# Decode attention with hand-written semaphores: TensorE's chunks as turns of one loop, V in one fixed buffer

## The chip, the cores and the metric

One core of a Trainium2 chip. The metric is the device time of one execution in microseconds (us), the median over runs; lower is better. "Before" is the kernel as it was, "changed" the rewritten one. The profile counts 16 DMA engines for the core, and the trace records 16 increments of each load's semaphore; each is taken here as the moment at which one engine's part of the load has arrived, and is called a landing. VectorE is DVE in the profile, ScalarE is ACT, GpSimd is POOL, and SP is the engine that issues most loads.

## The reference, cut to what matters

```python
def _A_ref(x, k_cache, v_cache, wq, wo):             # one token, D = 448
    q = (x @ wq) ...                                  # 16 heads of 256; 8 K/V heads, 65536 positions
    scores = einsum("bhqd,bhkd->bhqk", q, k) * (256 ** -0.5)
    p = softmax(scores)
    o = einsum("bhqk,bhkd->bhqd", p, v)
    return o @ wo
def _B_ref(x, w1, b1, w2, b2): ...                    # a small token mixer with gelu
return g * a + (1 - g) * b                            # g: one sigmoid gate
```

K and V are bf16, 8 x 65536 x 256 each: 2 x 268 MB, read once. Everything else is small (Wq and Wo are 3.7 MB each).

Of the kernel before, what the change touches and what calls it, by code (L numbers as in the profile page):

```python
# [21 lines left out]
RING = 3  # L22
MAXS = max(SIZES)


PAD = MAXS - 1
# [6 lines left out]
GELU_C1 = 0.044715  # L33


@with_exitstack
def kernel(
# [24 lines left out]
    assert DR == 64 and D % 4 == 0 and F % 128 == 0 and SK % (128 * SB * sum(SIZES)) == 0  # L62
    sizes = SIZES * (SK // (128 * SB * sum(SIZES)))
    n_chunks = len(sizes)
    n_steps = HKV * sum(sizes)
    scale = 1.0 / (DH ** 0.5)

    ctx.enter_context(tc.manual_schedule())


# [3 lines left out]
    work = ctx.enter_context(tc.tile_pool(name="work", bufs=1))  # L74
# [3 lines left out]
    ring = [ringp.tile([128, MAXS * SB * DH], BF16, name=f"ring{i}") for i in range(RING)]  # L78

    sc = [psum.tile([128, 512], FP32, name=f"sc{i}") for i in range(2)]  # L80
    pv = [psum.tile([128, 512], FP32, name=f"pv{i}") for i in range(2)]
    misc = psum.tile([128, 512], FP32, name="misc")
    den_ps = psum.tile([128, 512], FP32, name="den_ps")

    acc = psum.tile([128, 512], FP32, name="acc")


    total = HKV * n_chunks

    def piece(item, j, n):  # L90
        i, is_v = divmod(item, 2)
        g, c = divmod(i, n_chunks)
        nb = sizes[c] * SB
        lo = sum(sizes[:c]) * SB * 128
        src = (A_v_cache if is_v else A_k_cache)[0, g, lo:lo + 128 * nb, :]
        src = src.rearrange("(p j) d -> p (j d)", j=nb)
        nc.sync.dma_start(
            out=ring[item % RING][:, j * DH:(j + n) * DH], in_=src[:, j * DH:(j + n) * DH]
        )

    def load(item):
        last = sizes[-1]
        if item < 2 * total - 2:
            piece(item, 0, sizes[item // 2 % n_chunks] * SB)
        elif item == 2 * total - 1:

            for s in range(last):
                piece(item - 1, s * SB, SB)
            for s in range(last - 1):
                piece(item, s * SB, SB)  # L110
            piece(item, (last - 1) * SB, SB - TAIL)
            piece(item, last * SB - TAIL, TAIL)



    wq_slot = ring[RING - 1]
    wqa = wq_slot[:, 0:KA * HQ * DH].rearrange("p (k n) -> p k n", k=KA)
    wqb = wq_slot[:, KA * HQ * DH:KA * HQ * DH + 8 * DH]
    nc.sync.dma_start(
        out=wq_slot[:, 0:KA * HQ * DH], in_=A_wq[0:DA, :].rearrange("(p k) n -> p (k n)", k=KA)  # L120
    )
    nc.sync.dma_start(out=wqb, in_=A_wq[DA:D, :].rearrange("r (hh n) -> (r hh) n", hh=2))
    for item in range(RING - 1):
        load(item)


    x_row = const.tile([1, D], BF16)
    nc.scalar.dma_start(out=x_row[:], in_=A_x[0])
    gw_row = const.tile([1, D], BF16)
    nc.scalar.dma_start(out=gw_row[:], in_=gate_w.rearrange("(o n) -> o n", o=1))  # L130
    w1T = const.tile([128, NF], FP32)
    nc.gpsimd.dma_start(out=w1T[:], in_=B_w1[0, :].rearrange("(p b) -> p b", b=NF))
    b1T = const.tile([128, NF], FP32)
    nc.gpsimd.dma_start(out=b1T[:], in_=B_b1.rearrange("(p b) -> p b", b=NF))
    w2T = const.tile([128, NF], BF16)
    nc.gpsimd.dma_start(out=w2T[:], in_=B_w2[:, 0].rearrange("(p b) -> p b", b=NF))
    zb = const.tile([1, 2], FP32)
    nc.gpsimd.dma_start(out=zb[:, 1:2], in_=B_b2.rearrange("(o n) -> o n", o=1))

    wo_t = [const.tile([128, 4, D], BF16, name=f"wo{i}") for i in range(2)]  # L140

    def load_wo(g):
        nc.gpsimd.dma_start(  # L143
            out=wo_t[g % 2][:],
            in_=A_wo[g * 512:(g + 1) * 512, :].rearrange("(q p) n -> p q n", p=128),
        )


    ident = const.tile([128, 128], BF16)
    make_identity(nc, ident[:])  # L150



    sel = const.tile([128, 4], FP32)
    classes = sorted(set(sizes), reverse=True)
    assert list(sizes) == sorted(sizes, reverse=True)
    pick = const.tile([128, 2, len(classes)], FP32)
    nc.gpsimd.memset(sel[:], 0.0)
    nc.gpsimd.memset(pick[:], 0.0)
    rows = [(sel[:], 4, -1, 32 * a) for a in range(4)]  # L160
    for k, size in enumerate(classes):
        rows += [(pick[:, :, k], 2, -16, 32 * a + s) for a in range(4) for s in range(size)]
    for t, w, step, row in rows:
        nc.gpsimd.affine_select(  # L164
            out=t, in_=t, compare_op=ALU.not_equal, fill=1.0, base=-row,
            pattern=[[step, w]], channel_multiplier=1,
        )
    block = const.tile([128, 4], FP32)
    nc.gpsimd.memset(block[:], 0.0)
    for a in range(4):  # L170
        nc.gpsimd.memset(block[32 * a:32 * a + 32, a:a + 1], 1.0)
    mhalf = const.tile([128, 1], FP32)
    nc.gpsimd.memset(mhalf[:], -0.5)

    pairs = const.tile([128, 2, 256], BF16)
    nc.vector.memset(pairs[:, 0, :], 0.0)
    nc.vector.memset(pairs[:, 0, 0:256:2], 1.0)
    nc.vector.transpose(out=pairs[:, 1, :].bitcast(FP32), in_=pairs[:, 0, :].bitcast(FP32))
    one_b = pairs[0:1, 1, 0:256:2]
    one_f = const.tile([1, 128], FP32)  # L180
    nc.vector.memset(one_f[:], 1.0)

    kT = [work.tile([128, SB * DH], BF16, name=f"kT{i}") for i in range(2)]
    p_t = [work.tile([128, 512], BF16, name=f"p{i}") for i in range(2)]
    pT_t = [work.tile([128, 512], BF16, name=f"pT{i}") for i in range(2)]
    den = [work.tile([128, n_chunks], FP32, name=f"den{i}") for i in range(2)]
    dsum = work.tile([128, len(classes)], FP32, name="dsum")
    rden = work.tile([128, 2], FP32, name="rden")
    pvs = work.tile([128, 512], FP32, name="pvs")
    oT = work.tile([128, 4], BF16, name="oT")  # L190
    half_g = work.tile([128, 1], FP32, name="half_g")
    bias = work.tile([128, 1], FP32, name="bias")
    res = work.tile([128, DQ], BF16, name="res")
    qT = const.tile([128, 2, HQ], BF16)
    qr = const.tile([128, 8, HQ], BF16)
    qw = [const.tile([128, 8, WIN], BF16, name=f"qw{i}") for i in range(2)]
    gate = const.tile([128, 2], FP32)

    for t in pv + qw:
        nc.vector.memset(t[:], 0.0)  # L200
    nc.vector.memset(acc[:, 0:DQ], 0.0)


    xd = const.tile([1, 2, 128], BF16)
    nc.vector.memset(xd[:], 0.0)
    for hh in range(2):
        nc.vector.tensor_copy(
            out=xd[:, hh, :].rearrange("o (r two) -> o r two", two=2)[:, :, hh],
            in_=x_row[:, DA:D],
        )  # L210
    x_ps = misc[:, 480:480 + KA + 2]
    for k in range(KA + 2):
        if k < KA:
            row = x_row[:, 0:DA].rearrange("o (p k) -> o p k", k=KA)[:, :, k]
        else:
            row = xd[:, k - KA, :]
        nc.tensor.matmul(x_ps[:, k:k + 1], lhsT=row, rhs=one_b[:, 0:1], start=True, stop=True)
    xT = const.tile([128, KA + 2], BF16)
    nc.vector.tensor_copy(out=xT[:], in_=x_ps)


    u_b = work.tile([128, D], FP32, name="u_b")
    xg = u_b[0:1, :]
    nc.vector.tensor_tensor(out=xg, in0=x_row[:], in1=gw_row[:], op=ALU.mult)
    nc.vector.tensor_reduce(out=zb[:, 0:1], in_=xg, axis=AXIS.X, op=ALU.add)
    z_ps = misc[:, 500:502]
    nc.tensor.matmul(z_ps, lhsT=one_f[:], rhs=zb[:], start=True, stop=True)  # L227
    nc.scalar.activation(out=gate[:, 0:1], in_=z_ps[:, 0:1], func=ACT.Exp, scale=-1.0)
    nc.scalar.activation(out=gate[:, 1:2], in_=z_ps[:, 0:1], func=ACT.Exp, scale=1.0)  # L229
    nc.vector.tensor_scalar(out=gate[:], in0=gate[:], scalar1=1.0, scalar2=None, op0=ALU.add)  # L230
    nc.vector.reciprocal(out=gate[:], in_=gate[:])
    nc.vector.tensor_scalar(
        out=half_g[:], in0=gate[:, 1:2], scalar1=0.5, scalar2=None, op0=ALU.mult
    )
    nc.vector.tensor_tensor(out=bias[:], in0=z_ps[:, 1:2], in1=gate[:, 1:2], op=ALU.mult)


    xb_ps = sc[0][:, 0:D]
    nc.tensor.matmul(xb_ps, lhsT=one_b, rhs=x_row[:], start=True, stop=True)
    stats = const.tile([128, nc.vector.BN_STATS_DIM], FP32)  # L240
    nc.vector.bn_stats(out=stats[:], in_=xb_ps)
# [57 lines left out]

    queries(0)  # L300
    load(RING - 1)
    load_wo(0)
    load_wo(1)


# [212 lines left out]
```

## The kernel before: what the change and the argument touch

Each K/V head is cut into 6 chunks of 6, 6, 5, 5, 5, 5 steps; a step is 16 x 128 positions. A chunk of K or V is one load of 5 or 6 MiB, all from SP's queue, into a ring of three buffers that K and V share. TensorE's stream is unrolled over all 48 chunks; a framework places the semaphores.

```python
RING = 3
ring = [ringp.tile([128, MAXS * SB * DH], BF16, name=f"ring{i}") for i in range(RING)]
...
# K and V alternate: item 2i is K of chunk i, item 2i+1 is V of chunk i
nc.sync.dma_start(out=ring[item % RING][:, ...], in_=src[:, ...])
...
for i in range(total):                       # 48 chunks, all unrolled
    g, c = divmod(i, n_chunks)
    for s in range(sizes[c]):
        turn(i, s, n)                        # VectorE transposes one step of K (128x2048 fp32 words)
        scores(i, s, n)                      # TensorE: 8 matmuls 128x512
        mixer(n)
        ...
    load(2 * i + RING)                       # V of i+1: its buffer is free after scores(i)
    softmax(i)                               # ScalarE exp, VectorE transpose
    for s in range(...):
        p_v(i, s)                            # TensorE: 8 matmuls 4x512
    load(2 * i + 1 + RING)                   # K of i+2: its buffer is free after p_v(i)
```

The last V arrives in pieces. The last of its five steps is multiplied in a "turned" form (weights from V, output 128x2), which adds to the folded p.V of all steps before it in PSUM. Then come Wo, a bias and the output.

The softmax here doesn't subtract the row's maximum and nothing guards it: scores larger than these inputs give would overflow.

## Time and profile before

| | before |
|---|---|
| time | 1273.83 us (3 runs, 1273.68 to 1273.90) |
| span of the profiled run | 1272.2 us |
| bytes moved | 544.90 MB, 428 GB/s over the span |
| busy: TensorE / VectorE / DMA queue of K and V | 57% / 49% / 98.5% |
| instruction blocks: 16384 bytes / second queue | 35 / 11 |
| landings of the last load (16 engines) | 1259.4 to 1267.6 us, mean 1263.5 |

The page of the kernel before, first its share of busy time, then DMA by fortieths of the span and by queue (packets, MB, share of 16 engines' span):

```profile
PE 723.6 (57%) x4552; PEld 285.1 (22%) x4552; DVE 626.8 (49%) x388; ACT 58.4 (5%) x149; POOL 78.5 (6%) x145
...
DMA  9999999999999999999999999999999999999997
GB/s 408 426 428 433 432 439 429 429 432 433 435 432 431 431 433 435 431 432 431 432 438 429 432 433 437 435 425 435 431 435 436 427 432 435 436 438 425 432 429 301
...
q1 hardware_dynamic: 15416, 540.55, 98.5%
q0 software_dynamic: 1376, 3.69, 0.8%
q8 instruction: 35, 0.57, 0.2%
q14 instruction: 11, 0.09, 0.0%
```

No compute engine is near its limit and the DMA engines are never idle. The 35 packets on q8 are instructions. And the last slice, 301 GB/s, is where the engines end one by one.

The end of the kernel before, in order of time (start us, duration, engine, source line, operation):

```profile
1265.25 0.81 PE L382 MATMUL pv<-ring,pT 128*4 128x512 bf16 x8 [0.26 <-DMA ring<-in_A_v_cache_dram]
...
1266.11 0.42 DVE L472 COPY pvs<-pv 128x256 f32<-128x256 f32 x1 [3.32 <-PE pv L382]
1266.57 0.38 ACT L473 ACTIVATE pvs<-pv 128x256 f32<-128x256 f32 x1 [5.69 <-DVE pvs L472]
...
1266.59 1.05 PE L414 MATMUL misc<-sel,pvs 128*128 128x2 f32 x8 [0.54 <-DVE pvs L472]
...
1267.51 0.97 PE L425 MATMUL misc<-pT,ring 128*128 128x2 bf16 x32
...
1269.51 0.65 SPq L485 DMA_DIRECT2D out_dram<-res  x1
```

The last piece lands at 1267.6 us; the output is issued 1.9 us after that landing.

### The profile page before, as it was taken

Reading aid. Unit: us, or ns where it says so; the run is one execution under the profiler, and the core shown is the slowest. Engines: PE = TensorE matmul, PEld = TensorE weight load, DVE = VectorE, ACT = ScalarE, POOL = GpSimd, SP = SyncE. Lnnn points to the kernel's source line nnn. Section 1 sums busy time; section 2 is a strip of 40 time slices with the busy share of each in tenths; the row PEclk is TensorE's granted clock in tenths of the full one; section 3 lists DMA queues with packets and bytes.
Section 4 is the critical chain, followed back from the end, with each engine's and each line's share of the span. In section 5 each row is a group of like instructions: output and inputs, shape, how many; then the busy total and the mean of one; then the engine's idle time right before and its main releaser. Section 6 shows DMA issues by size and latency. Waiting matters only on the chain.

```text
span 1272.2 us, 10454 instructions
## 1 busy us (share of the span) xinstructions
PE 723.6 (57%) x4552; PEld 285.1 (22%) x4552; DVE 626.8 (49%) x388; ACT 58.4 (5%) x149; POOL 78.5 (6%) x145
## 2 busy tenths in 40 slices
PE   1566556654666546564565646655465555665467
PEld 1222122221222112221222212222122212222123
DVE  2555354644555355453554445544455435544455
ACT  0000000000000000000000000000000000000000
POOL 4110101111011110110000000000000000000000
PEclk9978777888788877888778888888788887878778
DMA  9999999999999999999999999999999999999997
GB/s 408 426 428 433 432 439 429 429 432 433 435 432 431 431 433 435 431 432 431 432 438 429 432 433 437 435 425 435 431 435 436 427 432 435 436 438 425 432 429 301
DMA packets 16842, 544.90 MB, mean 428 GB/s; under 512 B 2202, under 2 KB 2332, under 8 KB 3484
## 3 DMA queue, kind: packets, MB, share of 16 engines
q1 hardware_dynamic: 15416, 540.55, 98.5%
q0 software_dynamic: 1376, 3.69, 0.8%
q8 instruction: 35, 0.57, 0.2%
q14 instruction: 11, 0.09, 0.0%
q10 hardware_dynamic: 4, 0.00, 0.0%
HBM read 544.22 MB, written 0.00 MB: 428 GB/s over the span
## 4 chain that ended last, share of the span: by engine, by line
DMA 63%; PE 17%; DVE 11%; issue 8%; ACT 1%; POOL 0%; DVEq 0%; ACTq 0%; SPq 0%; POOLq 0%
DMA ring<-in_A_k_cache_dram 59%; PE sc L359 12%; DVE kT L351 9%; PE pv L382 5%; DMA zb<-in_B_b_dram 2%; DMA ring<-in_A_v_cache_dram 2%; DVE pT L370 1%; ACT p L366 1%; PE den_ps L398 0%; PE misc L270 0%; DVEq L351 0%; PE acc L314 0%; PE misc L414 0%; PE misc L274 0%; PE misc L425 0%
## 5 line engine op out<-in xcount | busy, mean ns | idle before, releaser
L359 PE MATMUL sc<-kT,qw 128*128 128x512 bf16 x2048 | 575.7, 434 | 443.8 <-DVE kT L351 442.8
L351 DVE STREAM_TRANSPOSE kT<-ring 128x2048 f32<-128x2048 f32 x256 | 575.3, 2288 | 478.1 <-DMA ring<-in_A_k_cache_dram 396.1
L359 PEld LDWEIGHTS <-qw 128*128 128x128 bf16 x2048 | 215.5, 108 | 791.5 <-DVE kT L351 332.2
L382 PE MATMUL pv<-ring,pT 128*4 128x512 bf16 x2040 | 125.7, 395 | 62.1 <-DVE pT L370 61.8
L370 DVE STREAM_TRANSPOSE pT<-p 128x512 bf16<-128x512 bf16 x48 | 34.2, 712 | 130.9 <-ACT p L366 130.9
L382 PEld LDWEIGHTS <-pT 128*4 128x4 bf16 x2040 | 46.6, 89 | 135.0 <-DVE pT L370 81.7
L366 ACT ACTIVATE p<-sc 128x512 bf16<-128x512 f32 x48 | 28.7, 597 | 1037.6 <-PE sc L359 1037.6
L143 POOL DMA_DIRECT2D wo<-in_A_wo_dram x8 | 6.3, 790 | 549.7 <-PE acc L314 549.7
L333 POOL TENSOR_SCALAR t_b<-t_b 128x448 f32<-128x448 f32 x14 | 7.9, 564 | 224.8 <-ACT t_b L325 224.5
L336 POOL TENSOR_TENSOR t_b<-t_b,u_b 128x448 f32<-128x448 f32 x14 | 16.0, 1142 | 1.2
L343 POOL TENSOR_TENSOR gel<-t_b,u_b 128x448 bf16<-128x448 f32 x14 | 15.9, 1133 | 1.2
L339 POOL TENSOR_SCALAR t_b<-t_b,half_g 128x448 f32<-128x448 f32 x14 | 8.9, 636 | 106.9 <-ACT t_b L338 101.9
L414 PEld LDWEIGHTS misc<-sel,pvs 128*128 128x128 f32 x64 | 11.8, 258 | 3.7 <-issue 2.0
L398 PE MATMUL den_ps<-pick,dsum 128*128 128x2 f32 x32 | 4.8, 256 | 12.5 <-DVE dsum L390 12.5
L227 PE MATMUL misc<-zb,one_f 1*128 1x2 f32 x2 | 0.5, 342 | 19.7 <-DMA zb<-in_B_b_dram 19.7
L325 ACT ACTIVATE t_b<-h_bc,b1T,w1T 128x448 f32<-128x448 f32 x14 | 10.5, 751 | 4.7 <-DVE h_bc L257 4.7
L414 PE MATMUL misc<-sel,pvs 128*128 128x2 f32 x64 | 10.2, 281 | 0.5 <-DVE pvs L472 0.5
L329 POOL TENSOR_SCALAR u_b<-h_bc,w1T,b1T 128x448 f32<-128x448 f32 x14 | 10.0, 716 | 2.1 <-DVE qT L277 0.9
L230 DVE TENSOR_SCALAR gate<-gate 128x2 f32<-128x2 f32 x1 | 0.2, 169 | 18.9 <-ACT gate L229 18.9
L366 ACT ACTIVATION_READ_ACCUMULATOR p<-sc 128x1 f32 x48 | 9.3, 194 | 0.0
L164 POOL TENSOR_SCALAR_AFFINE_SELECT pick<-pick 128x2 f32<-128x2 f32 x44 | 8.6, 197 | 3.0 <-POOL pick L164 0.2
L338 ACT ACTIVATE t_b<-t_b 128x448 f32<-128x448 f32 x14 | 8.0, 572 | 13.4 <-POOL t_b L336 13.4
(75 smaller groups left out, 66.0 us busy)
## 6 DMA issues: line engine op xcount, KB each, us to landing
ring<-in_A_k_cache_dram SPq DMA_DIRECT2D x31, 5120.0 KB, 29.8
ring<-in_A_v_cache_dram SPq DMA_DIRECT2D x31, 5120.0 KB, 23.4
ring<-in_A_k_cache_dram SPq DMA_DIRECT2D x16, 6144.0 KB, 33.0
ring<-in_A_v_cache_dram SPq DMA_DIRECT2D x16, 6144.0 KB, 28.0
ring<-in_A_k_cache_dram SPq DMA_DIRECT2D x5, 1024.0 KB, 25.1
ring<-in_A_v_cache_dram SPq DMA_DIRECT2D x4, 1024.0 KB, 22.6
wo<-in_A_wo_dram POOLq DMA_DIRECT2D x8, 448.0 KB, 19.5
ring<-in_A_wq_dram SPq DMA_DIRECT2D x1, 3072.0 KB, 10.1
```

Source lines behind the costliest of these rows:

```text
L164: nc.gpsimd.affine_select(out=t, in_=t, compare_op=ALU.not_equal, fill=1.0, base=-row, pattern=[[step, w]], channel_multiplier=1,)
L325: nc.scalar.activation(out=t_b[:], in_=h_bc[:], func=ACT.Square, scale=w1T[:, b:b + 1], bias=b1T[:, b:b + 1],)
L329: nc.gpsimd.tensor_scalar(out=u_b[:], in0=h_bc[:], scalar1=w1T[:, b:b + 1], scalar2=b1T[:, b:b + 1], op0=ALU.mult, op1=ALU.add,)
L336: nc.gpsimd.tensor_tensor(out=t_b[:], in0=t_b[:], in1=u_b[:], op=ALU.mult)
L339: nc.gpsimd.tensor_scalar(out=t_b[:], in0=t_b[:], scalar1=1.0, scalar2=half_g[:, 0:1], op0=ALU.add, op1=ALU.mult,)
L343: nc.gpsimd.tensor_tensor(out=gel[:], in0=t_b[:], in1=u_b[:], op=ALU.mult)
L351: nc.vector.transpose(out=kT[n % 2][:].bitcast(FP32), in_=kn[:, s * SB * 128:(s + 1) * SB * 128])
L359: nc.tensor.matmul(sc[i % 2][:], lhsT=qw[g % 2][:, q, PAD - s:PAD - s + 128], rhs=kv[:, :, q // 2, :, q % 2], start=(s == 0 and q == 0), s ...
L366: nc.scalar.activation(out=p_t[i % 2][:], in_=sc[i % 2][:], func=ACT.Exp, scale=scale, accum_out=den[g % 2][:, c:c + 1],)
L370: nc.vector.transpose(out=pT_t[i % 2][:], in_=p_t[i % 2][:])
L382: nc.tensor.matmul(pv[g % 2][32 * a:32 * a + 4, :], lhsT=pT[:, k, :, s], rhs=vt[:, j * DH:(j + 2) * DH], start=first and k < 4, stop=last ...
L414: nc.tensor.matmul(o_ps[:, 2 * c:2 * c + 2], lhsT=pvs[:, lo:lo + 128], rhs=sel[:, 2 * half:2 * half + 2], start=(half == 0 and c == 0), st ...
```

## The change

The intent: TensorE's stream becomes one loop, so that its body is fetched once. This needs every TensorE semaphore to be the same in each turn (wait for 1, then subtract 1), fixed buffers (V always in one buffer, K in two, so K runs one chunk ahead of V) and p.V of the previous chunk inside the current chunk's scores. The diff replaces the whole schedule; its core:

```diff
-RING = 3
-    ring = [ringp.tile([128, MAXS * SB * DH], BF16, name=f"ring{i}") for i in range(RING)]
+    vbuf = ringp.tile([128, MAXS * SB * DH], BF16, name="vbuf")
+    kbuf = [ringp.tile([128, MAXS * SB * DH], BF16, name=f"kbuf{i}") for i in range(2)]
 ...
+        def load_k(i):
+            if i >= 2:
+                sp.wait_ge(s_s, cum[i - 1])          # scores of chunk i-2 done
+            sp.dma_start(out=kbuf[i % 2][:, 0:n], ...)
+        def load_v(i):
+            if i >= 1:
+                sp.wait_ge(s_pv, i)                  # p.V of chunk i-1 done
+            sp.dma_start(out=vbuf[:, 0:n], ...)
+        def load_wo(g): ... sp.dma_start(...)        # was the software queue of GpSimd
 ...                                                 # order: K0 K1 V0 Wo | K2 V1 K3 V2 ...
+        with nc.Fori(0, total - 1, 1, engines=[PE], head_slot={PE: 0}):
+            for s, b in plan[0:4]:
+                scores(s, b, s == 0, False)
+            with pe.If_lt(f_reg, 1):                 # not in the first turn
+                pe.wait_ge(s_pt, 1).then_inc(s_pt, -1)
+                pe.wait_ge(s_v, 16).then_inc(s_v, -16)
+                for s in range(4):
+                    p_v(vbuf, pT_t[0], s, s == 0, False)
+                with pe.If_lt(v_reg, big):
+                    p_v(vbuf, pT_t[0], 5, False, False)
+                p_v(vbuf, pT_t[0], 4, False, True).then_inc(s_pv, 1)
+            with pe.If_lt(c_reg, big):
+                scores(5, 2, False, False)
+            scores(4, 0, False, True)
+            ...                                      # once per head: o, Wo
```

Also: VectorE now folds p.V out of PSUM after every chunk (two operations), the small weights arrive as rows on ScalarE's queue, and the mixer's sum is kept by GpSimd. VectorE, ScalarE, GpSimd and SP stay unrolled.

## The prediction

> **What bounds it now.** The loads. The forty slices show the DMA engines at 9 tenths throughout and 425 to 439 GB/s between the first and last slice; the page counts 544.9 MB. A 40960-byte packet takes 1.52 us, 27.0 GB/s per engine; the K/V queue is busy for 98.5% of 16 engines' span. TensorE is busy 57%, VectorE 49%. The chain of waits is 63% DMA. Only bytes, idle or uneven DMA engines, the start and the tail can move the time.

> **Where a little is left.** By the trace's times of landing, the 16 parts of one load, one per engine, land within 0.75 us of each other at 11 us, 2.2 us at 100 us, 3.7 us at 500 us, 6.8 us at 1000 us and 8.2 us at the end: the last piece of V lands between 1259.4 and 1267.6 us, mean 1263.5. The slowest engine sets the end. The growth is in steps of 0.5 to 1.2 us, several next to one of the 35 packets of 16384 bytes on the instruction queue (0.57 MB, 0.98 us each, one engine each). [...]

> **What the change does.**
> 1. TensorE's loop: about 30 of the 35 blocks are no longer fetched. Mean gain 0.54 MB at 430 GB/s, 1.2 us; evenness: I expect the last load's landings to spread 2 to 4 us, so the last one comes about 4 us earlier in all (2 to 5.5).
> 2. Wo moves from the software queue (3.69 MB, 0.8%, 9.7 us of an engine) to the K/V queue in 1792-byte rows; such packets took 75 ns before, so 2048 of them cost 9.6 us: nothing.
> 3. V has one buffer, so V of i+1 waits for p·V of i, with only K of i+2 (12.1 us) left in the queue. From K of i+1 landing: four transposes and score steps, about 13 us where the clock starts at 0.5 (first step about 3.4 us, later ones 2.3), while V of i lands; p·V takes 2.3 us; so V of i+1 is issued at about 15.5 of 24.3 us. Slack about 7 us after latency and spread. I expect no bubble.
> 4. Branches: [...] No run shows it yet.
> 5. Start: q no longer waits for the b2 load (25.6 us); off the path, since K0 and K1 fill 40 us. A hand-over between engines before the first load, and one at the end: +0.3 us each, a guess.
> 6. Tail (last landing to end 4.6 us before): two chained folds of p·V and semaphore hops in place of two copies: +0.3 us.

> **Sum.** -4 +0.3 +0.3 +0.3: about -3 us of 1273.8. Predicted 1270.8 us, range 1267.0 to 1275.0. Faster by over 2%: 0.01; within 2%: 0.97; slower: 0.02.

> **What would show it.** Instruction queue at 3 to 6 blocks of 16384 bytes; last-load spread under 4 us; DMA still 430 GB/s in the middle; the issuing queue's wait for p·V ending while K of i+2 is in flight (V's issue to landing about 20 us).

> **What would make it wrong.** The loop refetches its block each turn (47 packets or more: no gain). TensorE stalls at the branch for over 7 us: DMA gaps, 47 times. The spread comes from something other than instruction fetches.

The sum came to about -3 us of 1273.8 us: -4 for the last landing, +0.3 each for start, end and tail. That the 35 packets are TensorE's stream was an assumption, which e1 tests.

## The result and the profile after

| | before | changed |
|---|---|---|
| time, median | 1273.87 us (4 runs, 1273.68 to 1274.04) | 1270.40 us (4 runs, 1270.04 to 1270.49) |
| span of the profiled run | 1272.19 us | 1268.71 us |
| landings of the last load: first, mean, last | 1259.4, 1263.5, 1267.6 | 1258.6, 1259.5, 1262.9 |
| last landing to issue of the output | 1.87 us | 2.87 us |
| issue of the output to the end of the span | 2.68 us | 2.95 us |

The ratio is 0.9973, with a 95% interval of 0.9958 to 0.9987. A ratio here is the mean time of one kernel's fast runs over that of the other's fast runs of the same rounds, so it is not quite the ratio of the medians. The gain is 3.5 us, clear of noise but within 2%.

The landings are read from the trace: it records for each load 16 increments of its semaphore, taken as one from each DMA engine. The table's terms close: the last landing is 4.75 us earlier, the tail 1.0 us and the end 0.27 us longer, together 3.48 us less span.

The page of the changed kernel, the same lines:

```profile
PE 713.1 (56%) x4364; PEld 278.3 (22%) x4364; DVE 673.9 (53%) x511; ACT 50.1 (4%) x127; POOL 76.7 (6%) x98
...
DMA  9999999999999999999999999999999999999996
GB/s 412 420 441 434 425 435 437 431 434 438 439 426 427 434 435 433 438 428 434 440 436 429 430 434 432 434 438 434 434 427 444 427 430 434 436 430 429 436 433 294
...
q1 hardware_dynamic: 16728, 544.22, 99.3%
q8 instruction: 4, 0.07, 0.0%
q14 instruction: 9, 0.07, 0.0%
```

The blocks on q8 fell from 35 to 4, and Wo's bytes moved from q0 to q1. TensorE is about as busy as before (56% and 57%) and VectorE more (53% and 49%); that was never where the time was.

One turn of the changed kernel, in order of time:

```profile
408.80 8.89 DVE L520 STREAM_TRANSPOSE kT<-kbuf 128x2048 f32<-128x2048 f32 x4 [7.13 <-DMA kbuf<-in_A_k_cache_dram]
411.26 8.93 PE L652 MATMUL sc<-kT,qw 128*128 128x512 bf16 x32 [11.06 <-PEq L648]
...
420.93 2.33 PE L663 MATMUL pv<-vbuf,pT 128*4 128x512 bf16 x40 [0.74 <-PEq L694]
423.19 1.92 PE L652 MATMUL sc<-kT,qw 128*128 128x512 bf16 x8
423.30 0.33 SPq L241 DMA_DIRECT2D vbuf<-in_A_v_cache_dram  x1
...
432.93 4.51 DVE L520 STREAM_TRANSPOSE kT<-kbuf 128x2048 f32<-128x2048 f32 x2 [6.35 <-DMA kbuf<-in_A_k_cache_dram]
```

A K chunk lands at 408.8 us, the next V is issued at 423.3 us, 14.5 us later, and the next K lands at 432.9 us: V is queued 9.6 us ahead of that landing. In this turn the queue does not run dry.

The end of the changed kernel, as the chain that ended last has it (start us, duration, what):

```profile
1258.05 2.73 PE pv L663 x22
1260.78 0.47 PE acc L764 x8
1261.26 0.68 PE pv L663 x6
...
1262.03 0.50 DVE og L543
...
1262.55 0.50 DVE og L547
...
1263.15 0.63 PE misc L672 x4
1263.78 0.84 PE misc L783 x32
```

The last piece lands at 1262.9 us, but the turned matmuls (L783) start after the fold: two dependent VectorE operations of 0.5 us, hops between engines (0.1 us from VectorE's end at 1263.05 us to TensorE's start), then the turn (L672, four records, 0.63 us). They end at 1264.6 us, 1.7 us after the landing; before, it was 0.8 us.

### The profile page after: what moved, and what is told of

The parts are those of the page before. It is cut to its first block, busy times and chain, and to the rows that moved or that the text cites. A ratio compares the mean times of both kernels' runs of the same rounds, so it can differ in the third digit from the quotient of the medians.

```text
span 1268.7 us, 10632 instructions
## 1 busy us (share of the span) xinstructions
PE 713.1 (56%) x4364; PEld 278.3 (22%) x4364; DVE 673.9 (53%) x511; ACT 50.1 (4%) x127; POOL 76.7 (6%) x98
## 5 line engine op out<-in xcount | busy, mean ns | idle before, releaser
L652 PE MATMUL sc<-kT,qw 128*128 128x512 bf16 x2048 | 565.0, 438 | 463.9 <-PEq L648 463.9
L520 DVE STREAM_TRANSPOSE kT<-kbuf 128x2048 f32<-128x2048 f32 x256 | 571.2, 2283 | 328.1 <-DMA kbuf<-in_A_k_cache_dram 292.2
L652 PEld LDWEIGHTS sc<-kT,qw 128*128 128x128 bf16 x2048 | 213.8, 108 | 813.5 <-issue 649.6
L663 PE MATMUL pv<-vbuf,pT 128*4 128x512 bf16 x2008 | 129.2, 409 | 57.2 <-PEq L694 56.8
L573 DVE STREAM_TRANSPOSE pT<-p_t 128x512 bf16<-128x512 bf16 x48 | 34.1, 711 | 95.0 <-ACT p_t L599 95.0
L543 DVE SCALAR_TENSOR_TENSOR og<-pv,mask,og 128x256 f32<-128x256 f32 x39 | 18.9, 483 | 115.3 <-PE pv L663 115.3
L663 PEld LDWEIGHTS pv<-vbuf,pT 128*4 128x4 bf16 x2008 | 50.5, 91 | 133.9 <-issue 93.9
L599 ACT ACTIVATE p_t<-sc 128x512 bf16<-128x512 f32 x48 | 28.7, 597 | 1192.7 <-PE sc L652 1192.7
L547 DVE SCALAR_TENSOR_TENSOR og<-pv,mask,og 128x256 f32<-128x256 f32 x47 | 22.7, 484 | 1.7
L629 POOL TENSOR_TENSOR t_b<-t_b,u_b 128x448 f32<-128x448 f32 x14 | 15.8, 1127 | 1.2
L634 POOL TENSOR_TENSOR t_b<-t_b,u_b 128x448 f32<-128x448 f32 x14 | 15.8, 1126 | 1.2
L635 POOL TENSOR_TENSOR ymix<-ymix,t_b 128x448 f32<-128x448 f32 x14 | 15.8, 1126 | 1.1
L672 PEld LDWEIGHTS misc<-mask,og 128*128 128x128 f32 x32 | 4.9, 195 | 2.9 <-DVEq L773 1.9
```

Source lines behind the costliest of these rows:

```text
L520: ins = dve.transpose(out=kT[b][:].bitcast(FP32), in_=kn[:, s * SB * 128:(s + 1) * SB * 128])
L543: chain(dve.scalar_tensor_tensor(out=og[:], in0=pv[:, 0:DH], scalar=mask[:, M0, 0:1], in1=og[:], op0=ALU.mult, op1=ALU.add,))
L547: chain(dve.scalar_tensor_tensor(out=og[:], in0=pv[:, DH:2 * DH], scalar=mask[:, M1, 0:1], in1=og[:], op0=ALU.mult, op1=ALU.add,))
L573: ins = dve.transpose(out=pT[:], in_=p_t[:])
L599: ins = act.activation(out=p_t[:], in_=sc[:], func=ACT.Exp, scale=scale, accum_out=den[g % 2][:, c:c + 1])
L629: lambda: pool.tensor_tensor(out=t_b[:], in0=t_b[:], in1=u_b[:], op=ALU.mult),
```

## The experiments

Ten kernels ran, in three groups, each on one chip with its own runs of the kernel before (medians 1273.75, 1273.74, 1273.77 us). All gave a correct result. The changed kernel was not run again in these groups; the medians of the kernel before differ by at most 0.13 us between them, so times are set against it across groups. "Time" is the median of a kernel's runs, but everything read from a trace is of its one profiled run, which in some cases was not a typical one: 1273.62 us in e1 (the slowest of five), 1272.39 in e9 (the slowest), 1288.08 in e3b, 1273.59 in e4. "Mean" and "last" are of the 16 landings of the last load. "Idle" is worked out from the trace's packets between 30 and 1230 us: how far the number in flight was below 16, summed over time and divided by 16. "Lead" is the time from the issue of a V load to the landing of the K load ahead of it.

| run | time, us | mean | last | 16384 / 8192-byte instruction packets (q8 / q14) in the span | idle, us |
|---|---|---|---|---|---|
| before (profiled run) | 1273.87 | 1263.5 | 1267.6 | 35 / 11 | 0.0 |
| changed | 1270.40 | 1259.5 | 1262.9 | 4 / 8 | 0.0 |
| e1_unroll | 1272.95 | 1262.9 | 1266.4 | 35 / 8 | 0.1 |
| e2_wo_sw | 1270.11 | 1259.2 | 1262.7 | 4 / 8 | 0.0 |
| e3_nops | 1270.42 | 1259.4 | 1262.9 | 4 / 8 | not worked out |
| e6_two_blocks | 1270.36 | 1259.6 | 1262.9 | 4 / 8 | not worked out |
| e3b_waits | 1287.52 | 1275.4 | 1280.7 | 4 / 39 | 6.7 |
| e4_v_late | 1274.03 | 1264.3 | 1266.0 | 4 / 8 | 1.2 |
| e5_v_dry | 1411.5 | 1401.9 | 1403.2 | 4 / 8 | 94 |
| e7_tail | 1269.54 | 1259.7 | 1263.2 | 4 / 8 | 0.0 |
| e8_fold_group | 1268.65 | 1259.6 | 1262.2 | 4 / 7 | 0.0 |
| e9_waits_few | 1271.94 | 1260.9 | 1264.6 | 4 / 16 | 0.4 |

(The page of the changed kernel has 9 packets on q14; one of them is not an 8192-byte block.)

### e1: the loop undone

```diff
-        with nc.Fori(0, total - 1, 1, engines=[PE], head_slot={PE: 0}):
+        for i in range(total - 1):
+            c, v = i % PER, (i - 1) % PER
             ...same body; register tests become Python tests
```

> The changed kernel with TensorE's loop undone: the same 47 turns, in the same order with the same semaphores, written out one after the other. Theory (instruction fetches): the instruction queue is back at about 35 blocks of 16384 bytes, the mean of the last load's 16 landings comes 2 to 4 us later than 1259.5 us and their spread grows from 4.3 to 6 to 9 us, so the time is 1273 to 1275.5 us, at or above the kernel before. Rival (the gain came from the rest of the rewrite: other order of loads, Wo and small weights off the software queue): the time stays within 0.7 us of 1270.4 us although the blocks are back.

Measured: 1272.95 us (1272.71 to 1273.62, 5 runs), ratio to before 0.9994 (0.998 to 1.0007). Queues on the page:

```profile
q1 hardware_dynamic: 16728, 544.22, 99.2%
q8 instruction: 35, 0.57, 0.2%
q14 instruction: 8, 0.07, 0.0%
```

The gap between last and mean hardly moved: 3.56 us here, 3.44 in the changed kernel. That does not mean that TensorE's blocks delay all landings alike. In the changed kernel 15 of the landings lie within 2.0 us and one comes 2.3 us after them; here six lie from 1259.9 to 1260.4 us and eight from 1264.5 to 1266.4 us. Early loads of e1 spread by 2.1 us (at 287 us), later ones by 3.6 (431 us), 5.0 (718 us) and 6.2 us (1017 us), and the lengthening behind a block repeats with every eighth block (550, 551, 494, 498, 507, 468, 468, 481 ns, and from the start again). The trace does not name a packet's engine, so which engines carry the blocks is not shown. TensorE's blocks do make the landings uneven: 6.6 us from first to last with them, 4.3 without. The distance from mean to last hides it, because in the changed kernel a single landing is last, 2.3 us after the others (see e8).

Branches cost TensorE nothing that shows. In the list of groups, the last number is the idle time ahead of p.V; the changed kernel's line and then the unrolled one's:

```profile
L663 PE MATMUL pv<-vbuf,pT 128*4 128x512 bf16 x2008 | 129.2, 409 | 57.2 <-PEq L694 56.8
```

```profile
L663 PE MATMUL pv<-vbuf,pT 128*4 128x512 bf16 x2008 | 130.7, 412 | 60.0 <-PEq L687 59.7
```

It is 57.2 us with the loop's branches and 60.0 us without.

### e2: Wo back on the software queue

```diff
-            sp.dma_start(
+            pool.dma_start(              # waits and loads placed between GpSimd's mixer blocks
                 out=wo[:].rearrange("p r c n -> p r (c n)"), ...
```

> The changed kernel with only the eight Wo loads moved back to the software queue (issued by GpSimd). Theory as predicted (the queue does not matter, 3.67 MB cost the same engine time on either): within 0.5 us of 1270.4 us, mean landing of the last load within 0.5 us of 1259.5 us. Rival (software packets interleave with K/V packets and lengthen them: 40960-byte packets took 1515.6 ns before and 1514.3 ns after, 49152-byte ones 1820.3 and 1815.5, together about 1.8 us of an engine): 1.0 to 2.5 us slower, and those packet times are back at the values of before.

Measured: 1270.11 us (1269.79 to 1270.27). The mean landing is 0.2 us earlier, and K/V packets take 1514.5 and 1815.3 ns as in the changed kernel. The queue of Wo does not matter, as predicted; the rival falls.

### e3: no-ops on GpSimd (tested nothing)

```diff
+                for _ in range(50):
+                    pool.nop()                       # after each mixer operation
+        for _ in range(31 * 256 - 50 * turn):
+            pool.nop()
```

> The changed kernel with 7936 no-ops (31 blocks of 256) added to GpSimd's stream, which is idle 94% of the time and off the path; TensorE keeps its loop. Theory (what costs is the fetching of instructions by the DMA engines, whoever needs them): about 0.5 MB more on an instruction queue, last load's mean landing 1.5 to 4 us later, time 1272 to 1275 us. Rival (the loop itself, not the fetching, gains on TensorE): no change, within 0.5 us of 1270.4 us.

Measured: 1270.42 us, and exactly the instruction packets of the changed kernel (4 and 8), with no gaps between GpSimd's operations: 0.09 us from the end of one (403.72 us) to the next, where the waits of e3b leave 1.1 to 2.0 us. The no-ops did not reach the chip. (The 256 to a block in the expectation is what e3b then measured for waits.) An experiment that adds a cost must first show that the cost is there.

### e6: the loop body across two blocks

```diff
-        with nc.Fori(0, total - 1, 1, engines=[PE], head_slot={PE: 0}):
+        with nc.Fori(0, total - 1, 1, engines=[PE], head_slot={PE: 128}):
```

> The changed kernel with the loop's first instruction at slot 128 of a fetch block, so that the body lies across two blocks. If both blocks stay held between turns: 4 to 6 blocks of 16384 bytes on the instruction queue and 1270.4 us within 0.5 us. If a block is fetched again at each back edge: 47 or more blocks more, TensorE waits for each, time 1274 us or above. My expectation is the first.

Measured: 1270.36 us (1269.74 to 1270.76), 4 blocks on q8. Over 47 turns no block more was fetched than with the loop's head at slot 0, so the head's place is not what wins here. That the body then lies across two blocks is an estimate: the page of the kernel before counts 9104 matmuls and weight loads on TensorE against 35 blocks, about 260 to a block, and six steps of scores and six of p.V make 192 of them, which from slot 128 on reach past 260.

```profile
q8 instruction: 4, 0.07, 0.0%
```

### e3b and e9: instructions that must be fetched, on GpSimd

```diff
                 ins.then_inc(s_mp, 1)
+                for _ in range(50):                  # e9: only for the first 40 mixer operations
+                    pool.wait_ge(s_ma, 1)            # already satisfied
+        for _ in range(31 * 256 - 50 * turn):        # e3b only
+            pool.wait_ge(s_ma, 1)
```

> The run with no-ops showed no more bytes on the instruction queues than the changed kernel without them, so the no-ops never reached the chip and it tested nothing. The same again with 7936 instructions that must be executed: waits, in GpSimd's stream, on a semaphore that already has its value. Theory (the DMA engines' time for instruction blocks is what costs, whoever needs them; the unrolled run puts it at 3.4 us in the mean landing for 31 blocks of 16384 bytes): 0.5 MB more on an instruction queue, last load's mean landing 2 to 5 us later than 1259.5 us, time 1272 to 1275 us. Rival (the unrolled TensorE stream costs through TensorE's own pace): time within 0.5 us of 1270.4 us.

> The changed kernel with 2000 satisfied waits in GpSimd's stream instead of 7936, a quarter of the dose that cost 17 us. Theory (all of GpSimd's blocks burden one and the same DMA engine by about 0.57 us each, and that engine's landings then hold all others back): about 8 blocks of 8192 bytes more, one engine lands 2 to 5 us later, mean landing of the last load less than 1 us later than 1259.5, time 1271.5 to 1275 us. Rival (GpSimd's waits slow the kernel down some other way): the mean moves as much as the last landing, by about 4 us.

Measured for e3b: 1287.52 us (1286.68 to 1288.84), 13.8 us slower than before and 17 us slower than the changed kernel, for 31 more packets of 8192 bytes, 0.25 MB (7936 waits, so 256 to a packet).

```profile
q1 hardware_dynamic: 16728, 544.22, 98.6%
q14 instruction: 39, 0.32, 0.1%
```

The direction was right and the size wrong by a factor of five. A share of 0.1% of the DMA engines' time cost 1.3% of the kernel's. The landings show how. In e1 one engine is 1.8 us behind right after a fetch, and such a distance closes again (in the kernel before, 1.15 us at 328 us and 0.25 us at 373 us). In e3b a single engine falls behind all others: its distance to the next one grows from 0.6 us at 28 us to 5.6 us at 516 us. From then on it no longer grows steadily (4.7 to 9.2 us, 4.7 at the end), and the other engines go idle instead (6.7 us of idle, K/V packets 9.5 and 14.7 ns longer). So what these blocks cost shows at one landing of the 16. Its lag at 516 us, 5.6 us, is more than the shortest lead of V to a first landing in the changed kernel, 4.8 us. The kernel waits for all 16 landings of a load, so from there on the buffers come free late and the others wait with the last one: in all 17.8 us / 31 = 0.57 us per block in the last landing. The packets fit this: 0.31 us for a block and mostly 0.2 to 0.35 us more for the K/V packet behind it.

Measured for e9: 1271.94 us (1270.84 to 1272.39). While the waits run, one engine's distance to the next grows from 0.7 us at 71 us to 3.8 us at 581 us: again a single engine. It is not the one that is last in the changed kernel: the last landing but one is at 1262.9 us here, where the changed kernel has its last. That is why the last landing moved by only 1.7 us, just under the 2 to 5 us that I had expected. I had also expected the mean to move by less than 1 us, and it moved by 1.4. Idle of 0.4 us and a V lead to the first engine's landing of 1.4 us at its shortest (4.8 us in the changed kernel) show why: at a lag of 3 to 4 us the slow engine already holds the others back. The rival had the mean move by 4 us, which it did not either. What a lag costs thus depends on the slack, which the next two runs measure.

### e4 and e5: V later

```diff
                 sp.wait_ge(s_pv, i)
+                sp.wait_ge(s_e, i + 1)                                  # e4: exp of this turn done
+                sp.wait_ge(s_k[(i + 1) % 2], 16 * ((i + 1) // 2 + 1))   # e5 instead: next K landed
```

> The changed kernel with each load of V held back further: until the exponentials of the turn in which the buffer comes free are done, not only until its p.V is done (2.5 to 6 us later, by the trace of the changed kernel, in which V is issued about 9.6 us before the K ahead of it has landed). Theory (the single V buffer has slack): within 0.5 us of 1270.4 us. Rival (the queue must be two loads deep to keep the DMA engines busy): 0.5 us or more per turn, 1290 us or above.

> The changed kernel with each load of V issued only when the K ahead of it has landed, so that the queue runs dry once a turn. Both theories expect a loss; it measures what the end of the slack costs: [...]1340 to 1390 us, and a dip in the DMA engines' busy time once a turn.

Measured for e4: 1274.03 us (1273.23 to 1275.95), 3.6 us slower than the changed kernel. Neither theory's numbers hold. The median lead of V over the last landing of the K ahead of it is 9.6 us in the changed kernel and 7.0 us here. Counted to the first engine's landing, it is at least 4.8 us in the changed kernel, and under 3 us in 7 turns here, at the least 1.0 us. The loss shows as 1.2 us of idle and as longer K/V packets (1826.9 instead of 1815.5 ns for 49152 bytes, 1515.4 instead of 1514.3 ns for 40960 bytes: 3.5 us over 16 engines). So the single V buffer costs nothing as the kernel stands, but delays of 2.6 us at the median are more than its slack.

Measured for e5: 1411.5 us in its one run, more than the 1340 to 1390 us that I had expected: 141 us over the changed kernel, 3.07 us for each of 46 turns, the price of a queue that runs dry once. The stretches of 5 us (last three columns: granted clock, DMA share, GB/s) show a dip:

```profile
410.00:415.00 5.00, 4.29 (x28) 1.55 (x20) 0.97 (x2) 0.67 (x3) 0.00 (x0) 1.00 1.00 434
415.00:420.00 5.00, 0.00 (x0) 0.00 (x0) 2.73 (x2) 0.48 (x2) 3.62 (x4) 0.69 0.77 257
420.00:425.00 5.00, 4.56 (x14) 1.73 (x15) 5.00 (x4) 0.00 (x0) 0.00 (x0) 0.63 0.74 315
425.00:430.00 5.00, 4.14 (x20) 1.64 (x17) 4.18 (x2) 0.00 (x0) 0.00 (x0) 1.00 1.09 472
```

### e7: another tail

```diff
-        edges = [0, (steps[-1] - 2) * SB, (steps[-1] - 1) * SB, steps[-1] * SB - TAIL, steps[-1] * SB]
+        edges = [s * SB for s in range(steps[-1])] + [steps[-1] * SB - TAIL, steps[-1] * SB]
         ...
-        # p_v of steps 0..3, fold, o_turn; turned matmuls for step 4
+        # p_v of steps 0..2, fold, o_turn; turned matmuls for steps 3 and 4, each as its piece lands
```

> The changed kernel with another tail: the last V in six pieces instead of four, p.V of the last chunk folded after three steps, and two steps, not one, done in the turned form that needs no fold. In the changed kernel the last piece lands at 1262.9 us and its turned matmuls end at 1264.6 us, because the fold of the step before is still under way when the pieces land. Theory (the longer tail is that fold): the turned matmuls end 0.3 to 0.7 us after the last landing, so the time is 1269.0 to 1269.6 us. Rival (the tail is the hand-over between engines and the output): no change, 1270.4 us within 0.4 us.

Measured: 1269.54 us (1269.23 to 1269.62), 0.9 us faster than the changed kernel. The tail in order of time:

```profile
1259.03 0.48 DVE L543 SCALAR_TENSOR_TENSOR og<-pv,mask,og 128x256 f32<-128x256 f32 x1 [1.60 <-PE pv L663]
1259.54 0.48 DVE L547 SCALAR_TENSOR_TENSOR og<-pv,mask,og 128x256 f32<-128x256 f32 x1
1260.14 0.63 PE L672 MATMUL misc<-mask,og 128*128 128x2 f32 x4 [1.24 <-DVEq L775]
1260.74 0.98 PE L785 MATMUL misc<-pT,kbuf 128*128 128x2 bf16 x32
1262.62 1.01 PE L785 MATMUL misc<-pT,kbuf 128*128 128x2 bf16 x32 [0.90 <-DMA kbuf<-in_A_v_cache_dram]
```

The fold is over by 1260.8 us, TensorE waits for the piece, and its matmuls end at 1263.6 us, 0.4 us after the last landing (1263.2). The longer tail was the fold.

### e8: e7 and p.V folded once per head

```diff
             if 0 < i < total - 1:
-                dve.wait_ge(s_pv, i)
-                drain_pv((i - 1) % PER == 0)
                 if c == 0:
+                    dve.wait_ge(s_pv, i)
+                    drain_pv(True)
+                    chain(dve.memset(pv[:], 0.0))
 ...
-                    p_v(vbuf, pT_t[0], s, s == 0, False)
+                    p_v(vbuf, pT_t[0], s, False, False)
```

> The run with the other tail, and VectorE folds p.V once per head pair instead of once per chunk: 117 waits and folds fewer in its unrolled stream (7 memsets more). In the changed kernel one engine lands 2.3 us after all others at the end, and its lag grew in steps of 0.65 to 1.0 us at the times when 8192-byte blocks were fetched on the second instruction queue. Theory (VectorE's blocks all burden the same DMA engine): one block fewer, the lag of the last engine behind the next one is 0.5 to 1.0 us less than 2.3 us, time 1268.5 to 1269.1 us against 1269.5. Rival (the lag has another source): lag and time unchanged within 0.3 us.

Measured: 1268.65 us (1268.44 to 1268.72), ratio to before 0.996 (0.9946 to 0.9973). The second instruction queue has 7 blocks instead of 8:

```profile
q14 instruction: 7, 0.06, 0.0%
```

The theory held: the last engine is 1.27 us behind the next one at the end instead of 2.21 us in e7. In e7 as in the changed kernel its distance grew by 1.0 us between 901 and 914 us and again between 1177 and 1190 us, each time just after a block was fetched (at 905 and 1185 us); in e8 there is one such jump, between 1108 and 1121 us, just after a block at 1112 us. This is the fastest version, 5.1 us below the kernel before.

## Why the prediction was right or wrong

The time was predicted as 1270.8 us and measured as 1270.4 us; the change was predicted as about -3 us and was -3.5 us. The sum was right; two of its terms were not.

1. **The last landing** (predicted about 4 us earlier, 2 to 5.5; measured 4.75 us). That TensorE's instruction fetches are what is saved is shown by e1: putting them back, alone, moves the last landing by 3.5 us and the time by 2.55 us. The split was wrong. I had priced the bytes, "Mean gain 0.54 MB at 430 GB/s, 1.2 us", and left the rest to evenness. Measured, the mean moved by 4.1 us in all and 3.4 us by the loop alone (2.8 of it for the blocks), because a block of 16384 bytes costs an engine 1.44 us, not the 0.6 us of as many K/V bytes (an estimate, from 16384 bytes at the 27.0 GB/s of a 40960-byte packet). The distance from mean to last fell only from 4.1 to 3.4 us, and it did not change with the loop. The loop did make the landings more even: the first 15 of them lie within 2.0 us, and within 6.2 us when it is undone. What I had not reckoned with is the one engine that is last in the changed kernel, 2.3 us behind the rest; its lag grew by 1.0 us twice, just after 8192-byte blocks at 905 and 1185 us, which the loop leaves, and once only with a block fewer (e8). "I expect the last load's landings to spread 2 to 4 us" was just missed: 4.3 us.
2. **Wo's queue** (predicted: nothing). Right, by e2.
3. **The single V buffer** (predicted: V issued at about 15.5 of 24.3 us, no bubble). Right: 14.5 of 24.1 us in the turn shown, no idle. "Slack about 7 us after latency and spread" (an estimate: 24.3 less 15.5 us, less an allowance for these two) was wrong: the median lead is 7.3 us after the spread alone, 4.8 us at the shortest, and e4 spent all of the slack with 2.6 us at the median.
4. **Branches**. They did not show: TensorE is idle 57.2 us ahead of p.V with the loop's branches and 60.0 us unrolled (e1), and no block is fetched again, even with the head 128 slots later (4 blocks, e6). What one branch costs is not shown; in the turn shown TensorE is idle for 11.06 us ahead of the scores anyway.
5. **Start and end** (guessed +0.3 us each). The first packet of the K/V queue, one of Wq's, starts at 1.97 us instead of 1.75; the end after the output's issue is 0.27 us longer.
6. **Tail** (predicted +0.3 us, measured +1.0 us). The named cause was right, the two chained folds; e7, which takes them out of the way, wins 0.9 us. I counted the folds and not that the last pieces land while they run.

Two errors of size (mean landing too small, evenness too large) cancelled within one term; that the sum came out so close is luck.

What stays open: by the medians the unrolled run is 0.8 us faster than the kernel before although its tail is longer, and in its profiled run the mean landing is 0.7 us earlier; but the interval of the ratio (0.998 to 1.0007) does not exclude that there is no difference. If there is one, something else in the rewrite saves it (the small weights as rows and the other sizes of the last pieces are candidates); no run separates them. Why TensorE's blocks delay several landings (eight from 1264.5 to 1266.4 us in e1) and GpSimd's one (5.6 us behind the next in e3b) is not known either.

## What to carry to other kernels

Here, where the DMA engines are the limit (the K/V queue is busy 98.5% of the span), the instruction stream was traffic too: undoing the loop brought 31 blocks back and cost 2.55 us. Look at the instruction queues of the page, and price a block by an experiment or by its effect on the data packets, not by its bytes (1.44 us of an engine, not 0.6, in e1). Look at the 16 landings of the loads, not only at the mean rate: in e9 one late engine, 3.8 us behind the next at 581 us, cost 1.5 us for 8 more blocks, and in e3b, where its lag of 5.6 us had used up the lead with which loads are issued, 17 us for 31. The loop on TensorE, the engine with the longest stream, removed 31 of 35 blocks at no visible cost in branches (57.2 us idle ahead of p.V, 60.0 without them) and was not fetched again in 47 turns. What follows the last landing deserves a look of its own: e7 won 0.9 us there.
